# The factor 8 of a bias network moved into its evictions, and the last eviction moved from VectorE to ScalarE

## The chip, the cores and the metric

The kernel runs on one core of one Trainium2 chip. The metric is the time of one execution on the device in microseconds; before the change it is 659.53 us, the median of three runs (659.2 to 660.08).

## What is computed

Attention with a learned relative bias, followed by a feed-forward layer with a rational activation. Cut to what matters:

```
B, H, S, D = 4, 8, 576, 64                        # hidden = 32, d_model = 512, d_ff = 2048
scores = q @ k.T / sqrt(D)                        # for each batch and head
x = log1p(|i - j|) / log1p(max(i, 1))             # one number for each row i and column j
bias = relu(x * w1 + b1) @ w2                     # 32 hidden units, 8 heads
attn = exp(scores + bias - rowmax); attn = attn / (rowsum(attn) + 1e-9)
y = attn @ v                                      # heads joined: 2304 x 512
h = y @ w_in
g = (a0 + a1 h + a2 h^2 + a3 h^3) / (1 + |b0||h| + |b1| h^2 + 1e-6)
out = g @ w_out                                   # 2304 x 512
```

## The kernel before

The program has three stages, each an unrolled list of instructions that stands in the order in which the Python code records it. No scheduler reorders them: every engine works its own list from the front, and an instruction that waits holds up what is behind it on its engine.

**Bias network (lines 690 to 797).** The bias depends on i and on |i - j| alone, so it is computed once, for all four batches. The 576 rows are cut into 36 groups of 16, which are worked through in the order of the list `order`; its last three groups are 29, 28 and 27. For each group four relus (`relu`, line 730), shared between VectorE and ScalarE by the table `ENG`, write 32 hidden units for each of four rows into a ring of 18 buffers. TensorE then multiplies them with the weights `w28`, 32 columns at a time (line 765), into two banks of PSUM. An eviction multiplies the result with 1/log1p(i), which stands as a column of `rts`, and writes the block `e` (591 columns) into one of eight buffers of `rpool` (line 772). SyncE stores it to the table `tab` in device memory (line 781). `w28` is w2, laid out block by block, times 8: scores enter the softmax unscaled, and the reduction of line 356 multiplies with -0.125 = -1/(8) once for scores and bias together. The product with 8 is one GpSimd instruction at the start (line 711). With eight buffers the block of place y has to wait until the store of the block of place y - 8 has landed: group 27, the last, waits for group 31. Thirty-five blocks are evicted by ScalarE, the last, e27, by VectorE (line 776).

`load_bias` (line 251) reads parts of the table back, three DMAs for each part; these stand in SyncE's queue between the stores, and each waits until the rows that it reads have been stored.

**Attention (lines 242 to 688).** There are 72 steps (`steps`, line 318), each a chunk of 128 rows for two heads of a batch; 0 and 1 stand at the end of the bias network (`start`, line 654), and the others go two by two in rounds (`rnd`, line 589). A step consists of the scores on TensorE (`e_qk`, line 329, four products of two passes each into four banks), two reductions on VectorE, which add the bias and find the row maximum (`e_ttr`, line 346), two exponentials on ScalarE (`e_exp`, line 365, each followed by a read of its accumulator), transposes on TensorE (`e_tp`, line 410), copies of these out of PSUM on ScalarE, and the product with v (`e_pv`, line 474). A round records: scores of its two steps; the first step's reductions; the transposes of the two steps before; ScalarE's copies of them; the second step's reductions; products with v; the four exponentials. Of the transposes the first eight come from the earlier step, the next two are the rest of its row, and the eleventh and twelfth are the rest of the later step's row, for which both exponentials of that step have to be done. `side` (line 326) gives steps 0 and 1 the banks 4 to 7 and step 2 the banks 0 to 3; block e27 lies in banks 2 and 3 and block e28 in banks 0 and 1. So step 2's scores follow the eviction of e27.

**Feed-forward (lines 816 to 1011).** TensorE multiplies in two passes of high and low halves; the change touches nothing here.

At the start of the kernel `cpool` holds the constants: `cs` (one DMA, line 702), `w28`, and small tiles. The pools on the left side of memory are laid out behind it, one after the other: the tiles for incoming weights (`stg`), the bias tiles (`bpool`), and those of attention.

Of the kernel before, what the change touches and what calls it, by code (L numbers as in the profile page):

```python
# [9 lines left out]
F32 = mybir.dt.float32  # L10
F32R = mybir.dt.float32r
U32 = mybir.dt.uint32
AF = mybir.ActivationFunctionType
ALU = mybir.AluOpType
# [3 lines left out]
P = 128  # L18
B, H, S, D = 4, 8, 576, 64
NP = H // 2  # L20
HID = 32
# [3 lines left out]
NG = S // NROW  # L25
TW = 2 * S
EW = S + NROW - 1
# [10 lines left out]
def tile_attn_moe(  # L38
# [11 lines left out]
    V, A, G, T = nc.vector, nc.scalar, nc.gpsimd, nc.tensor  # L50

    cpool = ctx.enter_context(tc.tile_pool(name="cpool", bufs=1))
# [3 lines left out]
    cs = cpool.tile([P, NCST], F32, tag="cst", name="cst")  # L56
    w1s, b1s, abs_ = cs[:, 0:1], cs[:, 1:2], cs[:, 2:8]
    rts, pts = cs[:, 8:8 + NG], cs[:, 8 + NG:8 + 5 * NG]
    w28 = cpool.tile([P, 4 * HID], F32, tag="w28", name="w28")
    babs = cpool.tile([P, 2], F32, tag="babs", name="babs")  # L60
    qc = cpool.tile([P, 1], F32, tag="qc", name="qc")
    wmin = cpool.tile([P, 1], F32, tag="wmin", name="wmin")
# [32 lines left out]
    WF = W.rearrange("p a s -> p (a s)")  # L95
    used = deque(maxlen=600)

    def on(op, *banks, mem=()):
        banks, mem = frozenset(banks), frozenset(mem)
        for x, b, m in used:  # L100
            if not (banks & b or mem & m) and str(x.engine) != str(op.ins.engine):
                tc.declare_no_dep(op.ins, x, reason="other banks of PSUM, other tiles")
        used.append((op.ins, banks, mem))
        return op
# [127 lines left out]
    with tc.manual_schedule():  # L232
# [3 lines left out]
        with ExitStack() as actx:  # L236
# [24 lines left out]
            def load_qk(u, eng=nc.sync):  # L261
                p, b = units[u]
                t = qkp.tile([P, 2, S], F32, tag="qk", name=f"qk{u}", bufs=3)
                eng.dma_start(out=t, in_=qkt[b, p])
                qk[u] = (t[:, 0], t[:, 1])
# [99 lines left out]
            def e_exp(i, j):  # L365
                u, c = steps[i]
                if j == 0:
                    prob[i] = epool.tile([P, 2 * S], F32, tag="p", name=f"p{i}", bufs=2)
                t, m = s2.pop((i, j))
                k = 4 * j + c if c < 4 else 8 + j  # L370
                z = 1 - j
                A.activation(  # L372
                    out=prob[i][:, z * S:z * S + S], in_=t, func=AF.Exp,
                    bias=m, scale=-1.0, accum_out=sums[u % 4][:, k:k + 1],
                )
# [314 lines left out]
            with ExitStack() as bctx:  # L690
                tpool = bctx.enter_context(tc.tile_pool(name="tpool", bufs=1, side="right"))
                rpool = bctx.enter_context(tc.tile_pool(name="rpool", bufs=8, side="right"))
                ring = [bpool.tile([P, 10, S], F32, tag="bias", name="ring")]
                ring = [ring[0][:, x, :] for x in range(10)]
                ring2 = tpool.tile([P, 8, S], F32, tag="ring2", name="ring2")
                ring += [ring2[:, x, :] for x in range(8)]
                lts = tpool.tile([P, S], F32, tag="lts", name="lts")
                bts = tpool.tile([P, NG * 4], F32, tag="bts", name="bts")
                LCUT = 320
                warm = tpool.tile([P, P], F32, tag="warm", name="warm")  # L700
                V.memset(warm, 0.0)
                nc.scalar.dma_start(out=cs, in_=cst)
                nc.sync.dma_start(out=lts[:, :LCUT], in_=ltab[:, :LCUT])
                nc.sync.dma_start(out=lts[:, LCUT:], in_=ltab[:, LCUT:])
                for u in range(2):
                    load_qk(u)
                load_v(0)
                G.memset(qc, 1.0 + 1e-6)
                G.memset(wmin, -8.0 * 0x38000000)
                A.activation(out=bts, in_=pts, func=AF.Identity, scale=b1s)  # L710
                G.tensor_scalar(out=w28, in0=cs[:, 8 + 5 * NG:], scalar1=8.0, scalar2=None, op0=ALU.mult)
                V.tensor_scalar(
                    out=lts[:, :LCUT], in0=lts[:, :LCUT], scalar1=w1s, scalar2=None, op0=ALU.mult
                )
                A.activation(out=lts[:, LCUT:], in_=lts[:, LCUT:], func=AF.Identity, scale=w1s)
                for x in range(10):
                    on(T.matmul(W[:, 6, 0:P], warm, warm, start=True, stop=True), 6)  # L717

                def dist(n):
                    return max(NROW * n + NROW, S - NROW * n)  # L720

                ENG = [
                    "DDDD" if dist(n) > 432 else "DDDA" if dist(n) > 400 else "DDAA" for n in range(NG)
                ]

                rows = {}
                LEAD = 2
                nring = [0]

                def relu(n):  # L730
                    for c, e in enumerate(ENG[n]):
                        r = ring[nring[0] % len(ring)][:, :dist(n)]
                        nring[0] += 1
                        m = 4 * n + c
                        if e == "A":
                            A.activation(out=r, in_=lts[:, :dist(n)], func=AF.Relu, bias=bts[:, m:m + 1])
                        else:
                            V.tensor_scalar(
                                out=r, in0=lts[:, :dist(n)], scalar1=bts[:, m:m + 1], scalar2=0.0,
                                op0=ALU.add, op1=ALU.max,  # L740
                            )
                        rows[n, c] = r

                order = [16, 17, 0, 18, 1, 19, 2, 20, 3, 21, 4, 22, 5, 23, 6, 11, 7, 12]
                order += [8, 13, 9, 14, 10, 15, 32, 24, 33, 31, 34, 25, 35, 30, 26, 29, 28, 27]
                done = {16: 2, 19: 0, 26: 1}
                for n in order[:LEAD]:
                    relu(n)
                for y, n in enumerate(order):
                    if y == 13:  # L750
                        load_v(1)
                    if y + LEAD < NG:
                        relu(order[y + LEAD])
                    i0 = NROW * n
                    mid = i0 + NROW - 1
                    pa = 2 * ((y + 2 if y >= NG - 2 else y) % 4)
                    pa = (pa, pa + 1)
                    cuts = sorted({0, mid, 512, EW})
                    for a, z in zip(cuts, cuts[1:]):
                        b = pa[a // 512]  # L760
                        o = W[:, b, a % 512:a % 512 + z - a]
                        for c in range(4):
                            x = rows[n, c]
                            x = x[:, a - mid:z - mid] if a >= mid else x[:, mid - a:mid - z:-1]
                            on(T.matmul(  # L765
                                o[32 * c:32 * c + 32], w28[:, 32 * c:32 * c + 32], x,
                                start=True, stop=True,
                            ), b)
                    e = rpool.tile([P, EW], F32, tag="e", name=f"e{n}")
                    o = 512 * pa[0]  # L770
                    if y < NG - 1:
                        on(A.activation(
                            out=e, in_=WF[:, o:o + EW], func=AF.Identity, scale=rts[:, n:n + 1]
                        ), *pa)
                    else:
                        on(V.tensor_scalar(  # L776
                            out=e, in0=WF[:, o:o + EW], scalar1=rts[:, n:n + 1], scalar2=None, op0=ALU.mult
                        ), *pa)
                    g, k = divmod(n, 8)
                    x0 = S - NROW - i0  # L780
                    nc.sync.dma_start(
                        out=tab[g][NROW * k:NROW * k + NROW, :, x0:x0 + EW].rearrange("r h x -> (r h) x"),
                        in_=e,
                    )
                    if y in done:
                        load_bias(0, done[y])
                    if y == NG - 1:
                        load_bias(0, 4)
                        load_bias(0, 3)
                    if y == NG - 3:  # L790
                        start(0)
                    if y == NG - 1:
                        start(1)
                        for k in range(2):
                            for j in range(2):
                                e_exp(k, j)
                A.activation(out=babs, in_=abs_[:, 4:6], func=AF.Abs)

            wpool = ctx.enter_context(
# [16 lines left out]
        with ExitStack() as mctx:  # L816
            ep = mctx.enter_context(tc.tile_pool(name="ep", bufs=2, reuse_waits="tile"))
            xb = bpool.tile([P, 10 * S], F32R, tag="bias", name="xb")
            n = KD * TM
# [144 lines left out]
            for s in range(NQ + LAG + 1):  # L964
# [3 lines left out]
                n, fp = divmod(s, FPR)  # L968
# [121 lines left out]
```

## Time and profile before

| | |
|---|---|
| median of three runs | 659.53 us (659.2 to 660.08) |
| the profiled execution | 660.02 us |
| its span, by the profiler | 658.2 us |
| TensorE busy | 652.0 us (99%) |
| VectorE busy | 561.9 us (85%) |
| ScalarE busy | 470.9 us (72%) |
| GpSimd busy | 154.2 us (23%) |

In the rows below PE is TensorE (PEld its weight loads), DVE is VectorE, ACT is ScalarE, POOL is GpSimd, SP is SyncE, which issues the DMAs. A row of a timeline gives the start in us from the span's start, the duration in us, the engine, the line, the operation, the tile written and the tiles read, their shapes, and how many instructions are put together (x4); what stands in brackets is the idle time of the engine ahead of it and who ended it. TensorE's granted clock is 1.00, full speed, in all stretches.

### The profile page before, as it was taken

What the parts mean: (1) busy time and instruction counts of PE and PEld (TensorE: products, weight loads), DVE (VectorE), ACT (ScalarE), POOL (GpSimd) and SP (SyncE); (2) the same over time, 40 slices, a digit from 0 to 9 for tenths busy, and PEclk for the clock granted to TensorE, in tenths of its full rate; (3) what the DMA queues carried; (4) which work ended last, traced back from release to release, by engine and by line L of the source; (5) the groups of instructions that cost most, each with busy time, mean ns of one, the idle gap of its engine ahead of it and who ended that gap; (6) DMA issues with size and microseconds to landing.
All of it is one profiled execution on the core that took longest, in us unless ns stands there. A gap on an engine that the chain in (4) does not pass through costs nothing.

```text
span 658.2 us, 16142 instructions
## 1 busy us (share of the span) xinstructions
PE 652.0 (99%) x6276; PEld 549.1 (83%) x6276; DVE 561.9 (85%) x1100; ACT 470.9 (72%) x758; POOL 154.2 (23%) x109
## 2 busy tenths in 40 slices
PE   9999999999999999999999999999999999999997
PEld 7767888888888888988888888999988888888996
DVE  7997888988889995899999989989769779687776
ACT  8978999999999996768657565566655555555551
POOL 1000233433433331121221212212221221212211
PEclk9999999999999999999999999999999999999999
DMA  7888699798798864452725608669331301312031
GB/s 248 291 308 289 214 304 289 247 294 277 233 320 264 279 195 129 157 174 64 248 97 176 224 17 267 211 195 326 136 113 49 129 0 67 109 47 81 1 113 48
DMA packets 69901, 118.98 MB, mean 181 GB/s; under 512 B 9024, under 2 KB 30912, under 8 KB 69824
## 3 DMA queue, kind: packets, MB, share of 16 engines
q1 hardware_dynamic: 69680, 117.78, 54.3%
q8 instruction: 49, 0.80, 0.5%
q14 instruction: 28, 0.23, 0.1%
q10 hardware_dynamic: 144, 0.16, 0.1%
HBM read 79.17 MB, written 35.61 MB: 174 GB/s over the span
## 4 chain that ended last, share of the span: by engine, by line
PE 94%; DMA 2%; ACT 2%; DVE 1%; issue 1%; SPq 0%; DVEq 0%
PE ps L313 30%; PE ps L918 30%; PE ps L485 13%; PE ps L340 11%; PE ps L416 6%; PE ps L765 5%; DMA tab<-e 2%; ACT p L372 1%; ACT pt L431 1%; PE ps L717 1%; DVE s L356 0%; SPq L259 0%; DVE xl L298 0%; DVE e L776 0%; DVE pre L939 0%
## 5 line engine op out<-in xcount | busy, mean ns | idle before, releaser
L888 POOL TENSOR_TENSOR gl<-m,r 128x1024 fp32r<-128x1024 f32 (+1 forms) x39 | 85.6, 2195 | 299.5 <-DVE m L881 255.2
L839 ACT ACTIVATE w<-ps,babs 128x1024 f32<-128x1024 f32 (+1 forms) x40 | 41.3, 1032 | 107.6 <-PE ps L313 103.9
L372 ACT ACTIVATE p<-s,m 128x576 f32<-128x576 f32 x144 | 110.1, 781 | 1.2 <-DVE m L356 1.2
L356 DVE CUSTOM_DVE_ANT_0 s<-ps,bias 128x576 f32<-128x576 f32 (+1 forms) x144 | 95.1, 681 | 6.5 <-PE ps L340 3.4
L918 PE MATMUL ps<-wol,gh 128*128 128x512 f32 x216 | 84.2, 390 | 0.0
L918 PE MATMUL ps<-woh,gh 128*128 128x512 f32 x216 | 84.2, 390 | 0.0
L431 ACT COPY pt<-ps 128x512 f32<-128x512 f32 (+1 forms) x109 | 71.7, 731 | 16.2 <-PE ps L416 16.2
L340 PE MATMUL ps<-qk 64*128 64x288 f32 (+1 forms) x640 | 82.3, 418 | 0.5 <-DVE e L776 0.3
L851 DVE SCALAR_TENSOR_TENSOR u<-w,babs,ps 128x1024 f32<-128x1024 f32 (+1 forms) x40 | 46.9, 1172 | 38.1 <-ACT t L840 38.0
L485 PE MATMUL ps<-pt,v 128*64 128x128 f32 (+1 forms) x1280 | 78.4, 265 | 0.8 <-ACT pt L431 0.5
L485 PEld LDWEIGHTS ps<-pt,v 128*64 128x64 f32 x1280 | 65.3, 137 | 5.8 <-ACT pt L431 1.8
L313 PE MATMUL ps<-xb,wih 128*128 128x512 f32 (+1 forms) x240 | 68.8, 367 | 0.0
L340 PEld LDWEIGHTS ps<-qk 64*128 64x128 f32 (+1 forms) x640 | 50.8, 175 | 20.8 <-issue 5.6
L846 ACT ACTIVATE u<-u 128x1024 f32<-128x1024 f32 (+1 forms) x40 | 39.1, 977 | 40.3 <-DVE u L851 40.1
L416 PEld LDWEIGHTS ps<-ident,p 64*128 64x128 f32 x1296 | 50.3, 138 | 6.0 <-DVE m L356 0.6
L867 DVE SCALAR_TENSOR_TENSOR gh<-t,cst,r 128x1024 fp32r<-128x1024 f32 (+1 forms) x40 | 46.9, 1174 | 9.3 <-ACT r L848 6.9
L918 PE MATMUL ps<-woh,gl 128*128 128x512 f32 x216 | 53.8, 389 | 0.0
L416 PE MATMUL ps<-ident,p 64*128 64x64 f32 x1296 | 50.9, 226 | 0.1
L874 DVE SCALAR_TENSOR_TENSOR m<-u,qc,gh 128x1024 f32<-128x1024 f32 (+1 forms) x40 | 47.1, 1178 | 4.0
L313 PEld LDWEIGHTS ps<-xb,wih 128*128 128x128 f32 x240 | 44.5, 188 | 6.1
L881 DVE SCALAR_TENSOR_TENSOR m<-t,cst,m 128x1024 f32<-128x1024 f32 (+1 forms) x40 | 47.1, 1178 | 1.4
L860 DVE SCALAR_TENSOR_TENSOR t<-t,cst,ps 128x1024 f32<-128x1024 f32 (+1 forms) x40 | 47.0, 1174 | 1.4
(85 smaller groups left out, 1344.7 us busy)
## 6 DMA issues: line engine op xcount, KB each, us to landing
tab<-e SPq DMA_DIRECT2D x36, 295.5 KB
qk<-in_qkt_dram SPq DMA_DIRECT2D x16, 576.0 KB
wx<-in_w_in_dram SPq DMA_DIRECT2D x16, 512.0 KB
wx<-in_w_out_dram SPq DMA_DIRECT2D x16, 512.0 KB
v<-in_vp_dram SPq DMA_DIRECT2D x16, 320.0 KB
ws<-wh SPq DMA_DIRECT2D x20, 256.0 KB
ws<-wl SPq DMA_DIRECT2D x20, 256.0 KB
bias<-tab SPq DMA_DIRECT2D x16, 288.0 KB
```

What stands on the lines that cost most here:

```text
L313: on(T.matmul(hps[s][:, j, :w_], w[:, k, sl], x[:, k, :w_], start=(k == 0 and z == 0), stop=(k == KD - 1 and z == 2),), b + j)
L340: on(T.matmul(W[o, b, :SH], q[r, x], k[r, a * SH:(a + 1) * SH], start=True, stop=True), b)
L356: op = on(V.tensor_tensor_reduce(out=t3[:, a], in0=W[:, b:b + 2][:, a, :SH], in1=b3[:, a], scale=-0.125, scalar=least, op0=ALU.add, op1=AL ...
L372: A.activation(out=prob[i][:, z * S:z * S + S], in_=t, func=AF.Exp, bias=m, scale=-1.0, accum_out=sums[u % 4][:, k:k + 1],)
L416: on(T.transpose(W[:, b, o:o + 64], src[x, :], ident[x, x]), b)
L431: on(A.copy(out=t.rearrange("p x (r s) -> p r x s", r=2)[:, a:z], in_=W[:, to[a]:to[a] + z - a].rearrange("p r (x s) -> p r x s", s=64),), ...
L485: on(T.matmul(ps[y, o], vt[n][:, kc, y], w_, start=(kc == 0), stop=(kc == 4)), b, mem=(f"pt{i % 3}", f"tl{i // 2 % 2}"))
L860: on(V.scalar_tensor_tensor(out=rt[s, "t"], in0=rt[s, "t"], scalar=abs_[:, 1:2], in1=hp(s), op0=ALU.add, op1=ALU.mult,), *hb(s), mem="t")
L874: V.scalar_tensor_tensor(out=m, in0=rt[s, "u"], scalar=qc, in1=rt[s, "gh"].bitcast(F32), op0=ALU.add, op1=ALU.mult,)
L881: V.scalar_tensor_tensor(out=m, in0=rt[s, "t"], scalar=abs_[:, 0:1], in1=m, op0=ALU.add, op1=ALU.subtract)
L888: eng.tensor_tensor(out=lo, in0=rt[s, "m"], in1=rt[s, "r0"], op=ALU.mult)
L918: on(T.matmul(po[n, c], l[:, j, c * P:(c + 1) * P], r[fp][:, j, :], start=(first and x is a), stop=(last and x is z),), OB[c])
```

## The change

`w28` isn't a tile any more but the columns of `cs` that hold w2 as it came; GpSimd's product is gone. A new tile `rt8` (36 columns) holds 8/log1p(i); ScalarE computes it after the relus of the first two groups, and all evictions take their scale from it. The last block, e27, is evicted by ScalarE as the others are, recorded between the two exponentials of step 0, where all four exponentials of steps 0 and 1 stood behind the last eviction before.

```diff
-    w28 = cpool.tile([P, 4 * HID], F32, tag="w28", name="w28")
+    w28 = cs[:, 8 + 5 * NG:]
+    rt8 = cpool.tile([P, NG], F32, tag="rt8", name="rt8")
...
-                G.tensor_scalar(out=w28, in0=cs[:, 8 + 5 * NG:], scalar1=8.0, scalar2=None, op0=ALU.mult)
...
                 for n in order[:LEAD]:
                     relu(n)
+                A.activation(out=rt8, in_=rts, func=AF.Identity, scale=8.0)
...
-                    if y < NG - 1:
-                        on(A.activation(
-                            out=e, in_=WF[:, o:o + EW], func=AF.Identity, scale=rts[:, n:n + 1]
-                        ), *pa)
-                    else:
-                        on(V.tensor_scalar(
-                            out=e, in0=WF[:, o:o + EW], scalar1=rts[:, n:n + 1], scalar2=None, op0=ALU.mult
-                        ), *pa)
+                    if y == NG - 1:
+                        e_exp(0, 0)
+                    on(A.activation(
+                        out=e, in_=WF[:, o:o + EW], func=AF.Identity, scale=rt8[:, n:n + 1]
+                    ), *pa)
...
                     if y == NG - 1:
                         start(1)
-                        for k in range(2):
-                            for j in range(2):
-                                e_exp(k, j)
+                        for k, j in ((0, 1), (1, 0), (1, 1)):
+                            e_exp(k, j)
```

On ScalarE, at the end of the bias network, the evictions of the last blocks (`e29`, `e28`) stand ahead of the four exponentials (`p0` of step 0, `p1` of step 1), the small activation `babs` and the copies `pt0`, `pt1`. Before:

```order
L772 ACTIVATE e29_819<-ps_91,cst_61 128x591
L772 ACTIVATE e28_844<-ps_91,cst_61 128x591
L372 ACTIVATE p0_881,sum0_111<-s2_0_0_826,m0_0_0_827 128x576
L372 ACTIVATE p0_881,sum0_111<-s2_0_1_829,m0_1_0_830 128x576
L372 ACTIVATE p1_884,sum0_111<-s2_1_0_875,m1_0_0_876 128x576
L372 ACTIVATE p1_884,sum0_111<-s2_1_1_878,m1_1_0_879 128x576
L797 ACTIVATE babs_63<-cst_61 128x2
L431 COPY pt0_914<-ps_91 128x8x64 x2
```

The same place of the changed kernel:

```order
L774 ACTIVATE e29_819<-ps_91,rt8_62 128x591
L774 ACTIVATE e28_844<-ps_91,rt8_62 128x591
L373 ACTIVATE p0_860,sum0_111<-s2_0_0_826,m0_0_0_827 128x576
L774 ACTIVATE e27_859<-ps_91,rt8_62 128x591
L373 ACTIVATE p0_860,sum0_111<-s2_0_1_829,m0_1_0_830 128x576
L373 ACTIVATE p1_884,sum0_111<-s2_1_0_877,m1_0_0_878 128x576
L373 ACTIVATE p1_884,sum0_111<-s2_1_1_880,m1_1_0_881 128x576
L794 ACTIVATE babs_63<-cst_61 128x2
L432 COPY pt0_914<-ps_91 128x8x64 x2
```

One eviction, `e27`, has come between the first two exponentials, and three exponentials stand behind it.

On VectorE, at the same place, the last relus (`ring2`) are followed by the reductions of step 0 and step 1 (`s2_0_...`, `s2_1_...`, with the row minimum `m`). Before:

```order
L738 TENSOR_SCALAR ring2_126<-lts_127,bts_128 128x448 x4
L356 ISA s2_0_0_826,m0_0_0_827<-ps_91,bias0_489 128x576
L356 ISA m0_0_0_827 128x1
L356 ISA s2_0_1_829,m0_1_0_830<-ps_91,bias0_489 128x576
L356 ISA m0_1_0_830 128x1
L776 TENSOR_SCALAR e27_859<-ps_91,cst_61 128x591
L356 ISA s2_1_0_875,m1_0_0_876<-ps_91,bias0_489 128x576
```

The same place of the changed kernel:

```order
L738 TENSOR_SCALAR ring2_126<-lts_127,bts_128 128x448 x4
L357 ISA s2_0_0_826,m0_0_0_827<-ps_91,bias0_489 128x576
L357 ISA m0_0_0_827 128x1
L357 ISA s2_0_1_829,m0_1_0_830<-ps_91,bias0_489 128x576
L357 ISA m0_1_0_830 128x1
L357 ISA s2_1_0_877,m1_0_0_878<-ps_91,bias0_489 128x576
L357 ISA m1_0_0_878 128x1
```

The eviction that stood between the reductions of step 0 and those of step 1 is gone.

## Rows read from the trace of the kernel before

**Rows 1.** The page: the chain that ended last, share of the span by engine.

```profile
PE 94%; DMA 2%; ACT 2%; DVE 1%; issue 1%; SPq 0%; DVEq 0%
```

**Rows 2.** That chain in order of time up to 80 us: start, us, what.

```profile
43.35 5.18 DMA tab<-e
...
54.78 2.45 ACT p L372 x7
```

**Rows 3.** Busy us (instructions) in a stretch: PE, PEld, DVE, ACT, POOL; clock, DMA share, GB/s.

```profile
47.60:58.90 11.30, 10.40 (x140) 7.80 (x132) 8.28 (x27) 8.81 (x22) 0.00 (x0) 1.00 0.83 264
```

**Rows 4.** Timeline from 46 to 55 us, columns as told above.

```profile
46.81 0.75 ACT L772 ACTIVATE e<-ps,cst 128x591 f32<-128x591 f32 x1 [1.59 <-PE ps L765]
...
47.47 0.76 ACT L372 ACTIVATE p<-s,m 128x576 f32<-128x576 f32 x1
...
48.22 0.76 ACT L372 ACTIVATE p<-s,m 128x576 f32<-128x576 f32 x1
48.76 0.83 DVE L776 TENSOR_SCALAR e<-ps,cst 128x591 f32<-128x591 f32 x1 [1.33 <-DMA tab<-e]
...
49.51 0.75 DVE L356 CUSTOM_DVE_ANT_0 s<-ps,bias 128x576 f32<-128x576 f32 x1
...
49.64 2.34 PE L340 MATMUL ps<-qk 64*128 64x288 f32 x13 [0.29 <-DVE e L776]
...
50.30 0.78 ACT L372 ACTIVATE p<-s,m 128x576 f32<-128x576 f32 x1 [1.22 <-DVE m L356]
...
51.07 0.76 ACT L372 ACTIVATE p<-s,m 128x576 f32<-128x576 f32 x1
...
51.46 0.52 DVE L356 CUSTOM_DVE_ANT_0 s<-ps,bias,m 128x288 f32<-128x288 f32 x1
...
51.74 0.19 ACT L372 ACTIVATION_READ_ACCUMULATOR p<-s,m 128x1 f32 x1
51.83 0.19 ACT L797 ACTIVATE babs<-cst 128x2 f32<-128x2 f32 x1
...
52.05 1.39 PE L416 MATMUL ps<-ident,p 64*128 64x64 f32 x35
...
52.79 1.99 ACT L431 COPY pt<-ps 128x512 f32<-128x512 f32 x3 [0.77 <-PE ps L416]
```

**Rows 5.** Timeline of the start, 3.5 to 8 us.

```profile
3.14 1.92 PE L717 MATMUL ps<-warm 128*128 128x128 f32 x11
...
3.82 0.41 ACT L710 ACTIVATE bts<-cst 128x144 f32<-128x144 f32 x1 [1.80 <-DMA cst<-in_cst_dram]
3.87 0.61 POOL L711 TENSOR_SCALAR w<-cst 128x128 f32<-128x128 f32 x1 [1.83 <-DMA cst<-in_cst_dram]
...
4.54 1.88 ACT L736 ACTIVATE ring<-lts,bts 128x320 f32<-128x320 f32 x4
...
6.82 0.75 ACT L772 ACTIVATE e<-ps,cst 128x591 f32<-128x591 f32 x1 [0.41 <-PE ps L765]
```

**Rows 6.** Instructions reading `w28`: ns min/median/max, first and last start; their waits (us, times).

```profile
L765 PEld LDWEIGHTS ps<-ring,w x864: 106/109/123, 5.0 to 47.4; 128*32 128x32 f32 x173
...
  issue: 5.0, 24
```

**Rows 7.** Timeline of the next round, 55 to 59 us.

```profile
55.16 2.21 PE L340 MATMUL ps<-qk 64*128 64x288 f32 x16
...
57.60 0.20 ACT L372 ACTIVATION_READ_ACCUMULATOR p<-s,m 128x1 f32 x1
...
57.85 0.89 PEld L416 LDWEIGHTS ps<-ident,p 64*128 64x128 f32 x26 [0.24 <-ACT p L372]
...
58.30 1.07 ACT L431 COPY pt<-ps 128x512 f32<-128x512 f32 x2 [0.50 <-PE ps L416]
```

**Rows 8.** Timeline: VectorE at step 6 and at the first converted weights.

```profile
62.12 0.46 DVE L356 CUSTOM_DVE_ANT_0 s<-ps,bias 128x288 f32<-128x288 f32 x1 [0.37 <-PE ps L340]
...
67.54 0.42 DVE L155 TENSOR_SCALAR wk<-wx 128x512 uint32<-128x512 uint32 x1
```

## Prediction

> **What bounds the kernel now.** I read the chain that ended last by line first. It is TensorE for 94% of the span, and the DMA that stores bias blocks takes another 2% [rows 1]. So a part off TensorE counts only where TensorE waits, and the next view is where it does. The same chain in order of time shows one such place near the changed lines: a store of a bias block, issued at 43.35, holds the chain for 5.18 us, to 48.53, and later ScalarE holds it for 2.45 us from 54.78 [rows 2]. Busy time by stretch says what this handover from bias network to attention can give at all: from 47.6 to 58.9 TensorE is busy 10.40 of 11.30 us, so 0.90 us is the most [rows 3]. The timeline of that stretch gives the order of events [rows 4]. The last block, e27, needs the buffer whose store lands at 48.53; VectorE waits 1.33 us for it, evicts from 48.76 for 0.83 us, and only then takes the reductions of attention step 1 (from 49.51) and of step 2 (the second half of the first from 51.46). ScalarE, meanwhile, has done two exponentials (47.47, 48.22), sits idle 1.22 us until the third at 50.30, and starts the fourth at 51.07. The transposes resume at 52.05, released by VectorE's reduction of step 2, and ScalarE's first copy of them starts at 52.79. From there ScalarE runs without a gap worth naming into the exponentials of the next round. So the start of that copy, 52.79, is the time to follow.
>
> **The factor 8.** GpSimd's product of 128x128 goes (0.61 us, 3.87 to 4.48), and TensorE takes the first weights of the network at 5.0 [rows 5, 6], behind warm-up matmuls that run to 3.14 + 1.92 = 5.06 [rows 5]. GpSimd was not the last to be waited for, and the warm-up is unchanged: worth 0. The new instruction scales 36 columns on ScalarE after its first four relus, in a gap: these end at 4.54 + 1.88 = 6.42, and the first eviction waits for TensorE until 6.82, 0.41 us idle [rows 5]. Its price lies between 0.19 us (128x2, [rows 4]) and 0.41 us (128x144, [rows 5]); by columns 0.19 + 34/142 x 0.22 = 0.24 us. The gap hides it with 0.17 us left; without that cover it would cost its 0.24. I take 0, and keep 0 to 0.24. The 36 evictions have the same form as before, a scale from a column of a tile. TensorE's weights now come from inside the constants' tile; I take 0 for that and come back to it below.
>
> **The moved eviction.** On VectorE it disappears: 0.83 us, its idle 1.33 before it, and the place in front of step 1's reductions. On ScalarE it comes between the first two exponentials, where the third exponential's idle 1.22 us stands as cover. Behind it in ScalarE's queue are exponentials two to four and the copies; behind those wait TensorE's transposes. It waits for the same store as before, landing at 48.53. VectorE began 0.23 us after the landing; ScalarE has fewer waits to work off, and I take 0.15: start at 48.68. From an eviction to an exponential ScalarE needs 47.47 - 46.81 = 0.66 us, and one alone takes 0.75 [rows 4]; I take 0.70. So exponential two starts at 49.38 (1.16 later than now); three at 50.13, with 48.22 - 47.47 = 0.75; four at 50.89. Its accumulator is read out 51.74 + 0.19 - 51.07 = 0.86 us after its start: 51.75 instead of 51.93.
>
> What is late next? VectorE loses 0.83 us ahead of its reductions, so the one that now releases the transposes (51.46 + 0.52 = 51.98) ends near 51.1. TensorE's scores of step 2 start when e27 is out, 48.68 + 0.75 + 0.04 = 49.47 instead of 49.64; 14 of the 16 products of this round are left, at 2.21/16 = 0.138 us [rows 7] 1.93 us, so transposes begin near 51.4. They are issued in order, and the eleventh and twelfth need exponential four. So ScalarE becomes the last, as it is one round later: there the accumulator read ends at 57.60 + 0.20 = 57.80, TensorE goes on at 57.85 and ScalarE copies at 58.30, 0.50 us after [rows 7]. The same 0.50 here gives 51.75 + 0.50 = 52.25, against 52.79: **0.54 us earlier**. From both sides: if none of the transposes were done before the wait, they need 52.79 - 52.05 = 0.74 us after 51.80, which leaves 0.25; at most it is the 0.90 of [rows 3].
>
> Does it last? Behind the copy ScalarE is back to back, so the next round moves with it. What might stand still is DMA: the bias of step 6 is in time, since VectorE waits there for TensorE alone (0.37 us), and the first block of converted weights is read at 67.54 with no idle before it [rows 8]. Neither row says by how much the data were early; if by nothing, up to 0.54 is given back. The block's own store is issued some 0.2 us earlier. I let it last.
>
> **Sum.** 0 + 0 - 0.54 = -0.54 us. The profiled execution took 660.02 us, span 658.2 and 1.8 around it, so it would give 659.48; it lies 0.49 above the median of the runs, 659.53, from which I get 659.0.
>
> **Rivals.**
> *Given back* (chance 0.24). The copy starts earlier, but a later wait keeps its time: a bias or weight transfer that now lands just before it is read, or step 2's transposes. For it: the DMA engines are busy at 0.83 in this stretch [rows 3]. Against it: no wait of VectorE for a DMA in [rows 8]. Time: 659.5.
> *Slower transfers* (0.07). The tile that goes takes 512 bytes of each partition and the new one 144; built, the left-hand pools behind them, among them the bias tiles and the incoming weights, lie 352 bytes lower. [...] No row shows a transfer to two alignments. [...]
> *Earlier still* (0.08). The store lands before 48.2, so that ScalarE doesn't wait, or the scores run closer: up to the idle 0.90, 658.6. Against it: VectorE's 1.33 us of waiting [rows 4].
> *Slower weight loads* (0.06). The 864 weight loads of the bias network read 32 columns from 752 bytes inside the constants' tile instead of the start of an own one. One takes 109 ns, and from 5.0 to 47.4 they follow at 42.4/864 = 49 ns [rows 6], so they overlap about two deep. A load longer by x ns costs up to 864 x 0.45 x: 10%, 11 ns, is 4.3 us, 663.3. It outweighs the gain from 1.4 ns on. Against it: the loads' engine stood idle 24 times, 5.0 us, for no wait but its own issue [rows 6], so it isn't the limit.
> The forecast keeps 0.55.
>
> **How the numbers follow.** 659.0 is the likeliest. The forecast's bounds, 0.25 to 0.90, give 658.6 to 659.3, and the spread of the three runs, 659.2 to 660.08, another 0.4 to each side. "Given back" reaches 659.5 + 0.5. So 658.2 to 660.0 holds eight in ten. A measurement of this kernel tells about 0.2%, 1.3 us, from no change, and no case but the slower weight loads moves it so far: faster by more 0.06 (TensorE's whole idle time and a lucky spread), slower by more 0.06 (weight loads, and a slow tail of the transfers), within 0.88.
>
> **What would show it.** In the changed profile: ScalarE's eviction of e27 starts within 0.3 us of the store's landing; VectorE reduces step 1 before 49.2; exponential four starts 0.1 to 0.3 earlier; the first copy starts 0.3 to 0.7 earlier, released by transposes that waited for ScalarE and not for VectorE; rounds two to five start earlier by the same. The first eviction still starts at 6.8. Wrong if the copy moved and the round of 67 us didn't (given back), if the landing moved by more than 0.2 (transfers), or if a weight load takes other than 109 ns.

## The result, and the profile after

The changed kernel takes 665.87 us (median of 5 runs, 665.71 to 666.81) against 659.5 us of the kernel before beside it (659.2 to 660.08): ratio 1.0101, interval 1.0086 to 1.0116. It is 6.4 us slower; the forecast was 659.0. The profiled span grew from 658.2 to 664.0 us. Three slow executions, one of the kernel before (717.77 us), one of the kernel moved by 64 bytes (1300.85, the profiled one, so that no row of that kernel is read) and one of the eviction alone (3674.14), are left out of all ratios below.

I read the chain that ended last first, then the handover that the forecast followed, then the rest of the span. The chain by engine, of the changed kernel:

```profile
PE 97%; ACT 2%; issue 0%; DVE 0%
```

The DMA that held 2% of the chain before [rows 1] is gone; whether the change did that, the second profile of the kernel before tells, further down. The handover's busy time by stretch, columns as in [rows 3]:

```profile
47.60:58.90 11.30, 10.67 (x148) 8.52 (x146) 8.18 (x28) 10.04 (x24) 0.00 (x0) 1.00 0.89 279
```

TensorE is busy 10.67 us there, 0.27 more than before. The timeline of the same place, changed kernel:

```profile
46.77 0.76 ACT L774 ACTIVATE e<-ps,rt 128x591 f32<-128x591 f32 x1 [1.59 <-PE ps L766]
...
47.42 0.76 ACT L373 ACTIVATE p<-s,m 128x576 f32<-128x576 f32 x1
...
48.18 0.74 ACT L774 ACTIVATE e<-ps,rt 128x591 f32<-128x591 f32 x1
48.81 0.77 ACT L373 ACTIVATE p<-s,m 128x576 f32<-128x576 f32 x1
48.86 0.76 DVE L357 CUSTOM_DVE_ANT_0 s<-ps,bias 128x576 f32<-128x576 f32 x1 [1.48 <-PE ps L341]
...
50.44 0.76 ACT L373 ACTIVATE p<-s,m 128x576 f32<-128x576 f32 x1
...
50.83 0.52 DVE L357 CUSTOM_DVE_ANT_0 s<-ps,bias,m 128x288 f32<-128x288 f32 x1
...
51.41 1.25 PEld L417 LDWEIGHTS ps<-ident,p 64*128 64x128 f32 x35 [0.27 <-DVE m L357]
...
52.15 1.99 ACT L432 COPY pt<-ps 128x512 f32<-128x512 f32 x3 [0.77 <-PE ps L417]
```

ScalarE evicts e27 at 48.18, right behind the first exponential and with no wait: there is no idle time in the row. The first copy starts at 52.15 instead of 52.79, which is 0.64 earlier; the forecast was 0.54. What releases the transposes is still VectorE's reduction (the bracket of the 51.41 row), not ScalarE. In this pair of profiles the lead lasts: the next round's first copy comes at 57.65 instead of 58.30, and the first feed-forward product starts at 253.57 instead of 254.45. That is 0.88 earlier, more than the handover gave.

The loss is behind that. The last product of the kernel ends at 654.59 before and at 660.37 after, so the feed-forward stage took 400.14 us and takes 406.80, 6.66 more, at a granted clock of 1.00 in both. The chain of waits in order of time (start, us, what) shows it without any gap; a piece with x24 is 24 products back to back. Kernel before:

```profile
304.42 5.44 PE ps L313 x24
309.86 5.44 PE ps L918 x24
315.30 5.44 PE ps L313 x24
320.74 5.44 PE ps L918 x24
```

Changed kernel:

```profile
304.27 5.61 PE ps L314 x24
309.88 5.61 PE ps L915 x24
315.49 5.48 PE ps L314 x24
320.97 5.61 PE ps L915 x24
```

Twenty-four products take 5.61 us where they took 5.44: 234 ns each for 227. One of the four shown takes 5.48. Which ones are slow stands in the groups by line and shape (line, engine, operation, out<-in, shape, count | busy us, mean ns | idle before). In these rows the tile that is streamed, 512 columns, is named first, the one that is loaded as weights second; `xb` and `wg` lie in the two buffers that held the bias tiles. `xb` holds a part of the layer's input, `wg` a part of the weights of both its products; `gh` and `gl` hold the high and low halves of what the first product gives after the activation. Kernel before, feed-forward:

```profile
L918 PE MATMUL ps<-woh,gh 128*128 128x512 f32 x216 | 84.2, 390 | 0.0
...
L313 PE MATMUL ps<-xb,wih 128*128 128x512 f32 x144 | 44.4, 389 | 0.0
L918 PE MATMUL ps<-wg,gh 128*128 128x512 f32 x144 | 43.8, 389 | 0.0
...
L313 PE MATMUL ps<-xh,wih 128*128 128x512 f32 x72 | 28.0, 389 | 0.0
```

Changed kernel, the same:

```profile
L915 PE MATMUL ps<-woh,gh 128*128 128x512 f32 x216 | 85.4, 395 | 0.0
...
L314 PE MATMUL ps<-xb,wih 128*128 128x512 f32 x144 | 45.4, 396 | 0.0
L915 PE MATMUL ps<-wg,gh 128*128 128x512 f32 x144 | 43.9, 390 | 0.0
...
L314 PE MATMUL ps<-xh,wih 128*128 128x512 f32 x72 | 28.1, 391 | 0.0
```

The pattern is in the memory map as built. `w28` (512 bytes of each partition) went and `rt8` (144, laid out as 160) came, so every tile on the left side behind the constants lies 352 bytes lower, among them `xb`, `wg`, `gh`, `gl`. The tiles on the right side stayed: `xh`, `xl`, `wih`, `wil`, `woh`, `wol`. Before, all ten start at multiples of 256 bytes. After, the left ones start 160 bytes past such a multiple. Products with both tiles on one side take 389 to 391 ns, products across the sides 393 to 399. There are 936 products across the sides with 512 columns. From the start of one product to the start of the next, summed over the stage, these take 6.03 us more than before; the products of 512 columns within one side take 0.48 us more, and those of 384 columns 0.15. That is the 6.66.

### The profile page after: what moved, and what is told of

The parts are those of the page before. It is cut to its first block, busy times and chain, and to the rows that moved or that the text cites. A ratio compares the mean times of both kernels' runs of the same rounds, so it can differ in the third digit from the quotient of the medians.

```text
span 664.0 us, 16142 instructions
## 1 busy us (share of the span) xinstructions
PE 658.4 (99%) x6276; PEld 548.7 (83%) x6276; DVE 560.3 (84%) x1099; ACT 471.5 (71%) x760; POOL 153.8 (23%) x108
## 4 chain that ended last, share of the span: by engine, by line
PE 97%; ACT 2%; issue 0%; DVE 0%
PE ps L314 30%; PE ps L915 30%; PE ps L486 13%; PE ps L341 11%; PE ps L766 6%; PE ps L417 6%; ACT p L373 1%; ACT pt L432 1%; PE ps L717 1%; DVE pre L936 0%; ACT wh L165 0%; DVE tl L444 0%; DVE sum L384 0%; DVE warm L702 0%; DVE sum L383 0%
## 5 line engine op out<-in xcount | busy, mean ns | idle before, releaser
L915 PE MATMUL ps<-woh,gl 128*128 128x512 f32 x216 | 55.2, 395 | 0.0
L915 PEld LDWEIGHTS ps<-woh,gl 128*128 128x128 f32 x216 | 40.6, 188 | 9.8
L915 PEld LDWEIGHTS ps<-wol,gh 128*128 128x128 f32 x216 | 40.6, 188 | 9.4
```

Source lines behind the costliest of these rows:

```text
L915: on(T.matmul(po[n, c], l[:, j, c * P:(c + 1) * P], r[fp][:, j, :], start=(first and x is a), stop=(last and x is z),), OB[c])
```

## The experiments

The theory after the result: the loss is the place of the tiles and nothing else of the change ("place"). Its variants say what about the place counts: the distance between the two tiles of a product, or a tile's own address. The rivals: the eviction, the new weight loads, or the DMAs. `fill` is an otherwise unused tile behind the constants on the left, of 4 bytes an element; `fill2` one further behind, in front of attention's tiles; `edge` one on the right.

**The change with its tiles put back.**

```diff
-    fill = cpool.tile([P, 232], F32, tag="fill", name="fill")
+    fill = cpool.tile([P, 320], F32, tag="fill", name="fill")
```

> The changed kernel with its constants' pool made 352 bytes longer (the tile `fill` 320 columns instead of 232), so that all later tiles lie where they lay before the change. Theory 'place' (the loss of 6.4 us comes from the shift of the left-hand tiles, not from what the instructions do): the loss goes and the handover's gain stays, 658.8 to 659.2, feed-forward matmuls of 512 columns at 389 ns again. Rival 'weights' (the bias network's weights read from inside the constants' tile, or the moved eviction): nothing changes, 665.5 to 666.5, and matmuls keep 395 ns.

659.49 us, ratio 1.0 (0.9991 to 1.0009). The loss is gone, but the time lies above the 658.8 to 659.2 expected: the handover's gain isn't in it. A group of this kernel:

```profile
L915 PE MATMUL ps<-woh,gh 128*128 128x512 f32 x216 | 84.2, 390 | 0.0
```

The products are as before and so is the time. Both parts of the change are in it, and together they move nothing that the times can show; the interval reaches 0.6 us to either side.

**The kernel before with its tiles moved** as the change moves them: `fill` 144 instead of 232, nothing else.

> The kernel before with its constants' pool made 352 bytes shorter (`fill` 144 columns), and no other change. Theory 'place': 659.5 + 6.9 = 666.4 (6.4 measured plus the 0.6 of the handover that this kernel doesn't gain), matmuls with weights on one side and moving data on the other at about 395 ns. Rival 'weights': 659.5, as before.

666.15 us, ratio 1.0104 (1.0089 to 1.0118). Groups of this kernel:

```profile
L918 PE MATMUL ps<-woh,gh 128*128 128x512 f32 x216 | 85.4, 395 | 0.0
...
L313 PE MATMUL ps<-xb,wih 128*128 128x512 f32 x144 | 45.4, 396 | 0.0
```

The whole loss without the change. So "place" holds, and eviction and weight loads are out as its cause.

**Both sides moved by the same:** the change, with the right side 352 bytes lower as well.

```diff
-            G.memset(wpool.tile([P, 120], F32, tag="edge", name="edge"), 0.0)
+            G.memset(wpool.tile([P, 208], F32, tag="edge", name="edge"), 0.0)
```

> The changed kernel with the right-hand pools of the later stages lying 352 bytes lower too (the tile `edge` 208 columns instead of 120), so that left and right keep the distance they had before the change, though both have moved. Theory 'distance' (a matmul is slow when its weights and its moving data have shifted against each other): 658.8 to 659.4, all feed-forward matmuls at 389 ns. Rival 'own address' (a tile that doesn't start at a multiple of 256 bytes is slower to read): as slow as the changed kernel or slower, 665.5 to 668, with matmuls that read right-hand tiles on both sides slow too.

659.68 us, ratio 1.0003 (0.9994 to 1.0012). Groups of this kernel:

```profile
L915 PE MATMUL ps<-woh,gh 128*128 128x512 f32 x216 | 84.2, 390 | 0.0
...
L314 PE MATMUL ps<-xb,wih 128*128 128x512 f32 x144 | 44.3, 389 | 0.0
```

No tile of the stage starts at a multiple of 256 here, and every product is fast. It is the distance between the two tiles, not the address of either. The DMAs still write into left tiles that lie as in the changed kernel, so they are out as the cause too.

**The left side split:** the change with `fill2` 152 instead of 64, which puts `gh` and `gl` back and leaves `xb` and `wg` shifted.

> The changed kernel with the 352 bytes put back behind the bias tiles (the tile `fill2` 152 columns instead of 64): staging and bias tiles, among them xb and wg, stay shifted, everything behind them, among them gh and gl, lies as before the change. Theory 'distance': by pairs, woh or wol with gh and gl go back to 389 ns, xb with wih or wil stay at about 396, and wg with gh and gl, now shifted against each other, rise from 390 to about 395; altogether 661 to 663.5. Rival 'own address' of the moving tile: woh with gh unchanged at 395 and wg with gh at 390. Rival 'own address' of the weights: woh with gh at 389, wg with gh at 389, xb with wih at 389.

663.49 us, ratio 1.0062 (1.0048 to 1.0076). Groups of this kernel:

```profile
L915 PE MATMUL ps<-woh,gh 128*128 128x512 f32 x216 | 84.4, 391 | 0.0
...
L314 PE MATMUL ps<-xb,wih 128*128 128x512 f32 x144 | 45.4, 396 | 0.0
L915 PE MATMUL ps<-wg,gh 128*128 128x512 f32 x144 | 44.7, 396 | 0.0
...
L314 PE MATMUL ps<-xh,wih 128*128 128x512 f32 x72 | 28.0, 389 | 0.0
```

The slow groups changed as the distance says: `woh` with `gh` is fast again, and `wg` with `gh`, fast in the changed kernel, is slow, since now only one of the two is shifted.

**How far?** The kernel before with the left side 32, 64, 128 and 256 bytes higher: `fill` 240, 248, 264, 296.

> The kernel before with its constants' pool 32 bytes longer (`fill` 240 columns instead of 232): left-hand tiles 32 bytes further up, right-hand tiles where they were. The question is which distance matters. Theory '64': only whether left and right have shifted against each other by a multiple of 64 bytes counts (352 is 5 x 64 + 32): as slow as the shift by 352, 666.1, matmuls of 512 columns across the sides at about 395 ns. Rival 'how far': a small shift costs little, under 661. Rival '256': every shift that isn't a multiple of 256 costs, this one too, so it is e6 that tells these two apart.

> The kernel before with its constants' pool 64 bytes longer (`fill` 248 columns). Theory '64': no loss, 659.5, all feed-forward matmuls of 512 columns at 389 ns. Rival '256': about as slow as the shift by 352, 665 to 667. Rival 'how far': between the shift by 32 and that by 352.

> The kernel before with its constants' pool 128 bytes longer (`fill` 264 columns). Shifts by 32, 64 and -352 bytes have all cost 5 to 7 us, so the theory that only 64 counts has fallen. Theory '256': a shift by 128 costs as much, 664 to 666.5. Rival '128': nothing, 659.5, and matmuls of 512 columns at 389 ns.

> The kernel before with its constants' pool 256 bytes longer (`fill` 296 columns). Theory '256': no loss, 659.5, matmuls of 512 columns at 389 ns in all pairs. Rival 'any move' (the distance before the change is good by itself, or more than 256 bytes count): 664 to 667.

The ratios are 1.0092 (1.0076 to 1.0107) for 32 bytes, 1.0079 (1.0064 to 1.0095) for 64, 1.0085 (1.0071 to 1.0099) for 128, and 1.0001 (0.9992 to 1.0011) for 256. Groups at 128:

```profile
L918 PE MATMUL ps<-woh,gh 128*128 128x512 f32 x216 | 85.5, 396 | 0.0
```

and at 256:

```profile
L918 PE MATMUL ps<-woh,gh 128*128 128x512 f32 x216 | 84.2, 390 | 0.0
```

Of the distances tried, 0 and 256 are free, and 32, 64, 128 and 160 (the shift of the change) all cost 0.8 to 1.0%. The theory that a distance of 64 would be free too has fallen.

**Each part of the change by itself,** with the tiles where they were before. The eviction alone is the moved eviction in the kernel before; the factor alone is `rt8` and the raw weights, with `fill` 320 and e27 left to VectorE.

> The kernel before with the last eviction moved to ScalarE between the first two exponentials, as in the change, but with `w28`, its product on GpSimd and `rts` as before, so that no tile moves. Forecast's step (0.54 us gained at the handover and kept): 658.8 to 659.1. Rival 'landing' (the gain is there only in an execution in which the store that e27 waits for lands late, as in the profile of before; with the store in time VectorE's eviction is hidden behind the scores of step 1): 659.3 to 659.6, no difference.

> The kernel before with the factor moved into the evictions' scales (no GpSimd product, weights read from inside the constants' tile, the small scaling on ScalarE), the last eviction on VectorE as before, and the constants' pool made longer so that no later tile moves. Theory 'place': 659.3 to 659.7, no difference. Rival 'slower weight loads': over 661.

659.57 us, ratio 1.0001 (0.9992 to 1.001), and 659.44 us, 1.0002 (0.9994 to 1.0011). The first lies above the 658.8 to 659.1 that the forecast's step would give. The timeline of the eviction alone:

```profile
46.57 0.76 ACT L773 ACTIVATE e<-ps,cst 128x591 f32<-128x591 f32 x1 [1.59 <-PE ps L765]
...
47.98 0.74 ACT L773 ACTIVATE e<-ps,cst 128x591 f32<-128x591 f32 x1
...
51.95 1.99 ACT L431 COPY pt<-ps 128x512 f32<-128x512 f32 x3 [0.77 <-PE ps L416]
```

From the eviction of e28 to the copy it needs 51.95 - 46.57 = 5.38 us. Before it was 52.79 - 46.81 = 5.98 [rows 4]. But the factor alone, with e27 on VectorE, needs 5.39 too. That called for a second profile of the kernel before.

**The kernel before once more,** unchanged, one execution.

> The kernel before once more, no change, for a second profile of it. Theory 'landing': the store that e27 waits for landed late in the first profile by the run, not by the program; here VectorE evicts e27 within 1.2 us of the start of e28's eviction on ScalarE and the first copy of transposes starts 5.4 us after that, as in the runs with the change, not 6.0. Rival: 1.9 and 6.0 us again.

659.32 us. Its timeline:

```profile
47.09 0.75 ACT L772 ACTIVATE e<-ps,cst 128x591 f32<-128x591 f32 x1 [1.59 <-PE ps L765]
...
48.10 0.83 DVE L776 TENSOR_SCALAR e<-ps,cst 128x591 f32<-128x591 f32 x1 [0.41 <-ACT e L772]
...
49.18 0.76 DVE L356 CUSTOM_DVE_ANT_0 s<-ps,bias 128x576 f32<-128x576 f32 x1 [0.24 <-PE ps L340]
...
52.47 1.07 ACT L431 COPY pt<-ps 128x512 f32<-128x512 f32 x2 [0.77 <-PE ps L416]
```

5.38 us again, with the eviction on VectorE. Here the store has landed in time: VectorE waits 0.41 us, not 1.33 [rows 4], the bracket names no DMA, and then it waits 0.24 us more for the scores of step 1. So VectorE's eviction lay beside the scores and cost nothing. The chain that ended last, of this same execution, holds no DMA either:

```profile
PE 97%; ACT 2%; issue 0%; DVE 0%
```

So the DMA's 2% in the first profile belonged to that execution, and its absence from the changed kernel's chain doesn't speak for the change. The first feed-forward product starts at 253.75 here, within 0.2 us of the changed kernel's 253.57; in the changed kernel with its tiles back it starts at 254.38. In the eleven other profiled runs that I read for it the interval is 5.38 or 5.39, with e27 on either engine; only the one execution that I forecast from has 5.98. Is the move worth nothing, then, when the store is late? One run answers that, the changed kernel with both sides moved. Its timeline:

```profile
47.48 0.75 ACT L774 ACTIVATE e<-ps,rt 128x591 f32<-128x591 f32 x1 [1.59 <-PE ps L766]
...
49.32 0.75 ACT L774 ACTIVATE e<-ps,rt 128x591 f32<-128x591 f32 x1 [0.34 <-DMA tab<-e]
...
52.86 1.99 ACT L432 COPY pt<-ps 128x512 f32<-128x512 f32 x3 [0.42 <-PE ps L417]
```

ScalarE waits for the store and starts e27 49.32 - 47.48 = 1.84 us after e28; in the first profile of before it was 48.76 - 46.81 = 1.95 [rows 4]. The copy still comes 5.38 after e28. So with the store late the move saves about 0.6, as forecast in kind, and with the store in time nothing; one execution of each was late, so how often that is stays open.

**Can the kernel before be laid out better?** The identity of the transposes and the constants of the bias network also lie at other distances from their partners. Two pads of 192 bytes, `fill` 136 and a wider `warm` bring them to multiples of 256 apart.

> The kernel before with the remaining pairs of tiles that TensorE reads together brought to the same place within 256 bytes: the identity (from 128 to 64, where the transposed probabilities lie), w28 and the second part of the ring (from 128 and 160 to 0, where the first part lies); pads keep all later tiles where they were. Theory '256' for the earlier stages too: transposes and bias network a little faster, 657.5 to 659.3. Rival 'too short to matter' (64 columns a transpose, columns of the network at any offset): 659.2 to 659.8, no difference.

659.37 us, ratio 1.0001 (0.9992 to 1.0009). Thirty-five transposes in a row take 1.39 us, as before [rows 4]: nothing to win there.

**Which weights count?** In the feed-forward stage of the kernel before, the weights of 1820 of 1824 products are loaded while the product ahead of them runs: a load takes a median of 188 ns and starts a median of 223 ns ahead of its own product. So the distance that counts could be that from a product's moving tile to its own weights or to the next ones. At the end of the changed kernel 256 extra products are added: for each of two moving tiles (`woh`, right; one in `xb`, left) 32 with weights from the right, 32 from the left, then 64 by turns.

```diff
+            lw, rw = xh[NR - 1][:, 0, 0:P], wih[0][:, 0, 0:P]
+            for bank, x in ((0, woh[0][:, 0, :]), (4, xh[NR - 1][:, 1, :])):
+                todo = [rw] * 32 + [lw] * 32 + [rw, lw] * 32
+                for i, w in enumerate(todo):
+                    on(T.matmul(
+                        W[:, bank, :], w, x, start=(i == 0), stop=(i == len(todo) - 1),
+                    ), bank)
```

> The changed kernel with 256 more matmuls of 512 columns at its end, in two blocks; their results go nowhere. In the first block the moving tile is a right-hand one (woh), in the second a left-hand one (xb); the weights of each block are 32 times wih (right), 32 times xb (left), and then wih and xb by turns 64 times. Theory 'next load' (slow is a matmul under which weights are loaded from a tile that isn't at the same place within 256 bytes as its moving tile): by turns, woh with wih (next weights xb) about 397 and woh with xb (next weights wih) 389. Rival 'own weights': the other way round, woh with wih 389 and woh with xb about 396. Rival 'both': both about 393.

> The same 256 matmuls behind the changed kernel with its later tiles put back (`fill` 320 columns). All theories: every pair at 389 ns, by turns as well as in a row; were the turns themselves slow, it would show here.

The second kernel is the same with `fill` 320. 722.51 us against 715.02. Groups of the first, moving tile `woh`, in three stretches: weights from `wih` (its side), from `xb` (the other), by turns:

```profile
L1015 PE MATMUL ps<-woh,wih 128*128 128x512 f32 x32 | 7.5, 391 | 0.0
...
L1015 PE MATMUL ps<-woh,xb 128*128 128x512 f32 x32 | 7.6, 395 | 0.0
...
L1015 PE MATMUL ps<-woh,xb 128*128 128x512 f32 x33 | 13.0, 394 | 0.0
L1015 PE MATMUL ps<-woh,wih 128*128 128x512 f32 x32 | 12.6, 394 | 0.0
```

Moving tile in `xb`: weights from the other side, from its own, by turns:

```profile
L1015 PE MATMUL ps<-xb,wih 128*128 128x512 f32 x32 | 7.6, 396 | 0.0
...
L1015 PE MATMUL ps<-xb 128*128 128x512 f32 x32 | 7.5, 390 | 0.0
...
L1015 PE MATMUL ps<-xb 128*128 128x512 f32 x33 | 12.9, 392 | 0.0
L1015 PE MATMUL ps<-xb,wih 128*128 128x512 f32 x32 | 12.6, 393 | 0.0
```

With the pad, in a row and by turns alike:

```profile
L1015 PE MATMUL ps<-woh,wih 128*128 128x512 f32 x32 | 7.4, 389 | 0.0
...
L1015 PE MATMUL ps<-woh,xb 128*128 128x512 f32 x33 | 12.8, 389 | 0.0
```

In a row the distance decides for either moving tile. By turns both kinds of product take about the same, between the two, as the rival "both" had it; neither the own weights nor the next ones alone explain that. The means hide one thing, which the changed kernel's feed-forward stage shows: where products within one side follow products across the sides, the first four to ten of them still start 224 to 241 ns apart, and most of the later ones 226 or 227. So what a product takes hangs on more than its own pair of tiles and the next weights. What it is about the distance that takes the time stays open.

## Why the prediction was wrong

**The factor 8, taken as 0.** The step that failed is the memory map that comes with this edit. Under "Slower transfers" I had seen that the left-hand tiles lie 352 bytes lower, and had taken it for a matter of transfers alone, at a chance of 0.07; of TensorE's products in the feed-forward stage, some 400 us of them, I had said that the change touches nothing there. That term is +6.66 us (unchanged kernel, tiles moved: ratio 1.0104; changed kernel, tiles back: 1.0). It falls on the engine that holds the chain for 94% of the span [rows 1], so nothing hides any of it. No row of before showed a product at two distances; but the shift was known, and a bound on its effect on the products of the engine that bounds belonged in the sum. The instructions themselves were priced rightly: `rt8` takes 0.22 us (0.24 forecast), inside the gap ahead of the first eviction, and the factor alone gives 659.44.

**The moved eviction, -0.54.** In the profiles compared it came out as -0.64, within the forecast, and that is luck: the store that e27 waits for landed in time, so there was no wait to begin with. The term priced a wait of 1.33 us that one execution of the kernel before happened to have; the next execution has 0.41, hidden beside the scores. With the store in time the move gives 0: the handover takes 5.38 us with it and without it, which says more than the ratio of the eviction alone (1.0001, within 0.1%); with the store late it gave 0.6, from one execution with the move and one without. "Earlier still" had the early landing, but took it for a mishap of the new kernel rather than the usual case of both. That ScalarE would become the last to release the transposes failed as well: VectorE's reduction does. VectorE reduces step 1 at 48.86 (before 49.2, as forecast); the fourth exponential comes 51.07 - 50.44 = 0.63 earlier, more than the 0.1 to 0.3 forecast, for want of the wait. The first eviction starts at 7.06, not 6.8, behind a warm-up that ended 0.6 later in this execution; by the eviction of e28 nothing is left of that.

**Does it last: not decided.** In the pair of profiles it does, 0.65 us in the next round and 0.88 at the first feed-forward product, and 6.66 - 0.88 = 5.8 is the growth of the span. But the unchanged kernel's second execution starts that product as early to 0.2 us, so most of the 0.88 is what the first execution of before had lost, and no whole time shows a gain.

**Slower weight loads: no.** 110 ns for 109 [rows 6]:

```profile
L766 PEld LDWEIGHTS ps<-ring,cst x864: 105/110/141, 5.6 to 47.4; 128*32 128x32 f32 x173
```

They end at 47.4 as before, and the factor alone costs nothing.

**Slower transfers: not seen.** The rows of `bias` and of `qk` moved from multiples of 256 bytes to 160 bytes past one, and the DMA records of the traces give the time of each piece written into them. Pieces of 4608 bytes (`qk`) take a median of 178 ns and pieces of 256 bytes (the last columns of bias rows) 18 ns, in the kernel before and in the changed kernel alike, and the unchanged kernel with moved tiles needs the same 5.38 us in the handover. No row of before showed a slower write; the chance of 0.07 was my guess.

**The sign.** Slower by over 0.2% had a chance of 0.06, from weight loads and slow transfers. The range, 658.2 to 660.0, holds the medians of all kernels here whose tiles are in place, 659.32 to 659.68, and none whose tiles are not (the two with extra products aside). That is owed to its width: the gain of 0.54 on which it is built shows in none of those that have the moved eviction.

## What to carry to other kernels

When an edit adds, drops or resizes a tile, compare the built addresses of everything behind it, and put whatever moved into the sum of the engine that bounds; here a pad of 352 bytes is worth 6.4 us and both intended edits nothing that the times show. In a stage bound by TensorE look at the distance between the start addresses of the streamed and the loaded tile of a product: in this kernel, with products of 512 columns of 4 bytes, multiples of 256 bytes cost nothing (ratio 1.0001 after a move by 256), and moves by 32, 64 and 128 bytes and by the 352 of the change gave 1.0079 to 1.0104. A `fill` tile that looks useless may be what does it. Before pricing a wait, look at a second execution: if the releaser is a DMA, its landing may be chance, as here, with a wait of 1.33 us in one execution and of 0.41, not for the DMA, in the next.

## What the hardware showed

A product of 128x128 by 512 columns takes 227 ns back to back when its two tiles start a multiple of 256 bytes apart, and 234 ns at a distance of 160 bytes, at a granted clock of 1.00 both times; no wait, no idle time and no longer weight load shows (a median of 188 ns in both). Products within one side have a little of it too behind products that cross the sides: 5.48 us for 24 instead of 5.44. Transposes of 64 columns show none: 35 in a row take 1.39 us with their identity 64 bytes past a multiple of 256 from their partner, as in the kernel before, and 1.39 at a multiple.

The place of one tile against the other is worth 1% of this kernel: the ratio is 1.0101 for the change and 1.0104 for the moved tiles alone. Why the distance takes time no run here shows.
